# Row statistics in three batches, 16-bit table angles and a filter transform by column halves, in a fused long-convolution and token-mixing kernel

## The chip, the cores and the metric

The kernel runs on one core of one Trainium2 chip. The metric is the device time of one execution in microseconds (us); for the kernel before the change it is the median of six runs.

## What is computed

The reference, cut to what matters (S = 2048 tokens, D = 640 channels, F = 1536 hidden units, inputs in bf16):

```python
x = A_q
g = sigmoid((x * gate_w).sum(-1, keepdims=True))
# branch a: short filter, product, long causal convolution along S by FFT
k_shift = sum_t  k_pad[:, t:t+S, :] * shift_k[:, 3-t]          # 4 taps
kv = k_shift * v
y  = irfft(rfft(kv padded to 2S) * rfft(ssm_k padded to 2S))[:S]
a  = q * (y + kv * ssm_D)
# branch b: a token-mixing MLP on the normalized rows
h = (x - mean(x)) / sqrt(var(x) + 1e-5)                        # over D
u = gelu(einsum("bsd,sf->bdf", h, w1) + b1)
b = (einsum("bdf,fs->bds", u, w2) + b2) transposed to (S, D)
out = g * a + (1 - g) * b
```

## The kernel before, in words

**The convolution.** The Fourier transform along S is done as matrix products with a table `FTB` of cosines and sines, which is made on the chip, and with additions between four residue classes p = 0..3 of the token index ("mixing"). The filter `ssm_k` comes in as channels x tokens. For each half h of the tokens TensorE transposes it in five blocks of 128 channels (`transp`, L841; 8 transposes of 128x128 for each block); ScalarE copies each block from PSUM into `wT` (L853). The forward transform of the filter, `fwd` (L857), then makes for each p and each of two frequency blocks k2 and each component c (cosine or sine) four products of 320 columns: two token blocks kt times two column halves ci. The two column halves lie in the two PSUM banks of a slot `pp`, and ScalarE evacuates both with one instruction of 128x640 into `C[h]` (L871). Since one evacuation covers all 640 channels, the first product needs all five blocks of `wT`. `fwd_even` (L873) does p = 0 and 2 of the second half. Later the same is done for kv (`kv`, L1006, from the transposed keys `KT`), then the products and the inverse transform (`inverse`, L1215).

**The table.** L793 to L814: GpSimd makes small index rows (`acol`, `brow`, and `dif` for the identity matrix `ident`); for each p, VectorE multiplies them into 512 32-bit angles (L806), adds 1024 for the cosine (L807), takes all 1024 angles modulo 4096 (L811), and ScalarE's Sin turns them into 1024 table entries (L813). `ident` is made at L798, the zeroing of `rows` at L799 is GpSimd's, and the `taps` copy at L801 and the small `cw`, `cc` (L822 to L839) bring constants into place. `cw` feeds the four GpSimd products `KF` (L974).

**The MLP.** `X` holds the 2048 rows as 16 tiles of 128x640 (four tiles p in each of four groups hk). For each tile VectorE takes statistics with two instructions of 320 columns and one that joins them (`ln_tile`, L916, rows named `stats` and `mv`); GpSimd turns variances into `rstd` with a power of -0.5 (`ln_scale`, L929); VectorE applies mean and rstd in place (`ln_apply`, L935). This goes in two batches: tiles 0 to 7 are scaled after the statistics of tiles 0 to 11, and tiles 8 to 15 after those of the last four (L959 to L972). The first MLP product (`m1`, L1077) has 12 output tiles ft; each accumulates over hk = 0..3, 8 products of 320 columns for each hk, and reads `X` and a third of w1 in `ring[0]` or `ring[1]`. The second (`m2`, L1115) follows. The memory of `ring[1]` first serves the angles `pint`, the raw keys `kn` and a rearranged copy `kp0`; the keys are rearranged on VectorE and then transposed by DMA into `KT` (`k_turn`, L747), and only after that does the second third of w1 go into `ring[1]`.

**What sets the order.** Nothing runs in the order of the source. `_Sched` (L326) takes each operation with an estimated duration, a priority (by default its place in the source; smaller goes first) and its dependences, plays the engines through, and emits a fixed order for each engine; on the chip each engine executes that order and waits for semaphores in it. `after` adds an order of starts without a wait. There are four PSUM slots, of which convolution work ("cv") may hold three and the MLP ("mlp") two (L335). `m1` and `m2` have the lowest priorities and so fill what the convolution leaves of TensorE. DMAs from SP are issued in one chain. `spin` (L787) puts products of zeros ahead of a step, to keep TensorE busy while it waits.

## Time and profile before

| | us |
|---|---|
| median of 6 runs | 182.64 (181.78 to 182.9) |
| the profiled execution, own time | 181.8 |
| its span, first to last instruction | 180.0 |
| busy: TensorE / VectorE / ScalarE / GpSimd | 173.3 / 171.4 / 116.9 / 43.6 |
| scaling of a tile of X (16 of them), mean of one | 0.444 |
| statistics of 320 columns (32), mean of one | 0.465 |
| filter evacuation 128x640 from PSUM, mean of one | 0.724 |

How to read it: "busy" of TensorE counts products whose ends are modelled and overlap, so a busy TensorE isn't one at its peak. A mean duration is that of one instruction seen alone; instructions in a row overlap a little, so ten evacuations of 0.724 us take 6.07 us. The span leaves out 1.8 us around the program. A row of the timeline has the start, the length, engine, line, output and inputs, the number of instructions merged into it, and in brackets the idle time before it and what ended it.

### The profile page before, as it was taken

The page shows a single profiled execution, that of the slowest core. Times are in us where ns is not written, and L with a number is a line of the kernel's source. Part 1 is how long each engine was busy: PE and PEld are TensorE (multiplying, and loading weights), DVE is VectorE, ACT ScalarE, POOL GpSimd, SP SyncE. Part 2 cuts the span into 40 slices and gives each one's busy share as a digit, 9 for nine tenths or more (in the row PEclk, how much of TensorE's full clock was granted, in tenths as well). Part 3 has the DMA queues.
Part 4 walks back from the last instruction along what each step waited for, and adds up shares of the span by engine and source line. Part 5 has one row for each costly group of instructions (what it writes and reads, how often), then busy time and mean ns, then how long its engine had stood idle before and what let it go on. Part 6 is the DMA issues. An engine that isn't in the chain of part 4 may idle for free.

```text
span 180.0 us, 3335 instructions
## 1 busy us (share of the span) xinstructions
PE 173.3 (96%) x1381; PEld 129.4 (72%) x1381; DVE 171.4 (95%) x203; ACT 116.9 (65%) x176; POOL 43.6 (24%) x42
## 2 busy tenths in 40 slices
PE   7969998999999999999999999999999999999994
PEld 2636786687778677777677778888888887777772
DVE  7999895999999999999999899999999999999984
ACT  5798998899898999616999933132131223753760
POOL 4089404190000054000240110402625000252000
PEclk9999999999999999999999999999999999999999
DMA  6999999999999999998299969798899999599464
GB/s 154 362 410 374 389 302 192 257 410 323 211 260 287 190 270 250 237 221 199 57 240 305 198 85 364 179 209 277 155 197 216 209 201 383 222 152 241 117 225 143
DMA packets 38542, 43.51 MB, mean 242 GB/s; under 512 B 15867, under 2 KB 31360, under 8 KB 38528
## 3 DMA queue, kind: packets, MB, share of 16 engines
q1 hardware_dynamic: 33296, 32.16, 58.4%
q0 software_dynamic: 5200, 11.14, 35.5%
q8 instruction: 11, 0.18, 0.4%
q10 hardware_dynamic: 32, 0.01, 0.0%
q14 instruction: 3, 0.02, 0.0%
HBM read 25.87 MB, written 2.62 MB: 158 GB/s over the span
## 4 chain that ended last, share of the span: by engine, by line
PE 88%; ACT 10%; DVE 0%; issue 0%
PE pp L295 88%; ACT wT L670 3%; ACT C L670 2%; ACT ksh L670 2%; ACT FTB L670 2%; ACT L670 1%; ACT GT L670 0%; DVE O L682 0%; DVE zz L686 0%; ACT cw L670 0%; DVE cst L686 0%
## 5 line engine op out<-in xcount | busy, mean ns | idle before, releaser
L295 PE MATMUL pp<-X,ring 128*128 128x320 bf16 x384 | 55.4, 299 | 0.0
L626 DVE TENSOR_TENSOR C<-C 128x2560 bf16<-128x2560 bf16 (+2 forms) x37 | 54.5, 1524 | 0.0
L295 PE MATMUL pp<-GT,W 128*128 128x320 bf16 x384 | 52.6, 299 | 0.0
L295 PEld LDWEIGHTS pp<-GT,W 128*128 128x128 bf16 x384 | 43.6, 114 | 8.6
L295 PEld LDWEIGHTS pp<-X,ring 128*128 128x128 bf16 x384 | 37.4, 98 | 14.4
L670 ACT ACTIVATE C<-pp 128x640 bf16<-128x640 f32 x64 | 40.4, 724 | 4.7 <-PE pp L295 4.7
L670 ACT ACTIVATE O<-pp,c,omg 128x640 bf16<-128x640 f32 x15 | 13.3, 883 | 34.7 <-PE pp L295 34.7
L264 POOL DMA_DIRECT2D C<-C x8 | 10.9, 1610 | 41.9 <-DVE C L626 38.4
L295 PE MATMUL pp<-wT,FTB 128*128 128x320 bf16 x112 | 17.2, 300 | 2.6 <-ACT wT L670 1.5
L670 ACT ACTIVATE cgb<-pp,gg 128x640 bf16<-128x640 f32 x16 | 12.7, 793 | 5.7 <-PE pp L295 5.3
L295 PEld LDWEIGHTS pp<-wT,FTB 128*128 128x128 bf16 x112 | 10.5, 98 | 7.8 <-ACT wT L670 1.9
L670 ACT ACTIVATE GT<-pp,cc 128x640 bf16<-128x640 f32 x12 | 9.5, 795 | 9.0 <-PE pp L295 9.0
L626 DVE TENSOR_TENSOR tm<-C,C 128x2560 bf16<-128x2560 bf16 (+1 forms) x7 | 14.3, 2059 | 0.0
L922 DVE BATCH_NORM_STATS2 stats<-X 128x6 f32<-128x320 bf16 x32 | 13.6, 465 | 0.0
L295 PE MATMUL pp<-C,FTB 128*128 128x320 bf16 x96 | 13.4, 299 | 0.0
L264 POOL DMA_DIRECT2D C<-q_hi x6 | 5.9, 977 | 27.7 <-DVE C L626 13.2
L295 PEld LDWEIGHTS pp<-C,FTB 128*128 128x128 bf16 x96 | 9.3, 98 | 3.8 <-issue 0.2
L670 ACT ACTIVATE gq<-gq 128x640 bf16<-128x640 bf16 x16 | 11.8, 739 | 0.0
L626 DVE TENSOR_TENSOR SS<-C 128x2560 bf16<-128x2560 bf16 x8 | 11.7, 1488 | 0.1
L626 DVE TENSOR_TENSOR C<-tm 128x2560 bf16<-128x2560 bf16 (+1 forms) x9 | 10.7, 1193 | 0.1
L670 ACT ACTIVATE wT<-pp 128x1024 bf16<-128x1024 f32 x10 | 9.7, 1045 | 1.0 <-PE pp L295 1.0
L670 ACT ACTIVATE ksh<-pp 128x1024 bf16<-128x1024 f32 (+1 forms) x12 | 9.8, 896 | 0.6 <-PE pp L295 0.6
(73 smaller groups left out, 194.2 us busy)
## 6 DMA issues: line engine op xcount, KB each, us to landing
ring<-in_B_w_dram SPq DMA_DIRECT2D x12, 512.0 KB, 7.9
W<-in_B_w_dram SPq DMA_DIRECT2D x12, 512.0 KB, 6.3
C<-C POOLq DMA_DIRECT2D x8, 640.0 KB, 10.5
X<-in_A_q_dram SPq DMA_DIRECT2D x4, 640.0 KB, 8.6
kn<-in_A_k_dram SPq DMA_DIRECT2D x4, 640.0 KB, 9.6
out_dram<-O SPq DMA_DIRECT2D x7, 320.0 KB, 3.4
C<-SS POOLq DMA_DIRECT2D x3, 640.0 KB, 11.6
ssm<-in_A_ssm_k_dram SPq DMA_DIRECT2D x3, 512.0 KB, 7.0
```

The source lines that it names most:

```text
L264: ins = engobj.dma_start(out_ap, in_ap, accum_op=ALU.add, max_dma_last_dim=2560)
L295: ins = self.nc.tensor.matmul(ps_ap, lhsT=lhsT, rhs=rhs, start=start, stop=stop, skip_group_check=True)
L626: o_ = SC.add(eng, d, lambda s: T.op(eng, lambda e: e.tensor_tensor(o, a, b, op), rd, [o]), rd, [o], prio=prio, name="tt")
L670: return T.op("ACT", lambda e: e.activation(o, src, func, **kw), rr + [src], ww)
L922: ops.append(SC.add("DVE", 0.38, (lambda o, i: lambda s: T.op("DVE", lambda e: e.bn_stats(o, i), [i], [o]))(o, i), [i], [o]))
```

## The change

- The angles are made from two 16-bit parts: `tb`, (acol x brow) modulo 4096 and the same plus 1024, made once for all p with 32-bit products of 128 elements, and `jrow`, the rest of the angle for each p and kt, written by eight GpSimd index instructions of 256 elements. For each p there is one 16-bit addition of 1024 elements and one 16-bit modulo of 1024 elements. `pint` becomes 16-bit.
- `ident` is made after the first p's angles; the zeroing of `rows` moves from GpSimd to VectorE; the priorities that held back the Sin of p = 1 and 3 are gone.
- The first half's filter transform (`fwd_c`) runs the column halves outermost: for ci = 0 all p, then ci = 1. The two components c take the two banks of a slot, and one evacuation of 128x640 covers both components of one column half. The counts of products (64) and evacuations (16) stay.
- Row statistics and scaling in three batches, tiles 0 to 7, 8 to 12 and 13 to 15, in one written order on VectorE: statistics of the next batch come before a batch is scaled, and the joining instruction of a tile stands between the two statistics instructions of the next.
- The scheduler's estimates: start times of the engines, DMA rates of the first loads, GpSimd's power (1.75 for 1.05) and index instructions, the transposes; index instructions, memsets and the power no longer take part in its model of the port that VectorE and GpSimd share. The product `sd` x `rstd` loses its priority, and `KF` no longer waits for the last angles.

```diff
--- before.py
+++ after.py
...
@@ -397,9 +400,9 @@
         engs = list(ENGS) + ["SP", "QA"]
         ready = {e: [] for e in engs}
         pend = {e: [] for e in engs}
-        free = {e: 2.4 if e == "ACT" else 0.0 for e in engs}
+        free = {"ACT": 2.93, "DVE": 0.85, "POOL": 0.83, "PE": 1.18, "SP": 0.0, "QA": 0.0}
         port = {"DVE": 0.0, "POOL": 0.0}
-        dma_free = 0.0
+        dma_free = 0.3
         avail = {}
         for op in ops:
             avail[op] = 0.0
@@ -582,8 +585,10 @@
         C = [alloc(f"C{i}", [128, 4, 4, D], BF16) for i in range(4)]
         SS = alloc("SS", [128, 2, 4, D], BF16)
         E_base = cur[0]
-        acol = alloc("acol", [128, 2, 4], I32, at=base_of(SS))
-        brow = alloc("brow", [128, 2, 128], I32, at=base_of(SS) + 64)
+        acol = alloc("acol", [128, 1], I32, at=base_of(SS))
+        brow = alloc("brow", [128, 128], I32, at=base_of(SS) + 64)
+        prod = alloc("prod", [128, 128], I32, at=base_of(SS) + 64 + 2048)
+        tb = alloc("tb", [128, 2, 2, 128], I16, at=base_of(SS) + 64 + 2560)
         dif = alloc("dif", [128, 128], I32, at=base_of(SS) + 64 + 1024)
         dif2 = alloc("dif2", [128, 32], I32, at=base_of(SS) + 64 + 1536)
         KT = [alloc(f"KT{i}", [128, NG, KTW], BF16) for i in range(2)]
@@ -597,7 +602,8 @@
         rows = alloc("rows", [20, 5, 512], BF16, at=base_of(GT))
         kn = [alloc(f"kn{i}", [128, 4, D], BF16, at=base_of(ring[1]) + 5120 * i) for i in range(2)]
         kp = [alloc("kp0", [128, NG, 128], BF16, at=base_of(ring[1]) + 10240), alloc("kp1", [128, NG, 128], BF16, at=base_of(GTB))]
-        pint = alloc("pint", [128, 4, 2, 2, 256], I32, at=base_of(ring[1]))
+        pint = alloc("pint", [128, 4, 2, 2, 256], I16, at=base_of(ring[1]))
+        jrow = alloc("jrow", [128, 8, 256], I16, at=base_of(ring[1]) + 8192)
         W2 = alloc("W2", [128, 32, 512], BF16, at=base_of(ring[0]))
         assert base_of(ring[1]) == base_of(ring[0]) + 16384
         O1 = alloc("O1", [128, 4, 4, D], BF16, at=base_of(X))
@@ -682,8 +688,13 @@
                 return T.op("DVE", lambda e: e.scalar_tensor_tensor(out=o, in0=src, scalar=sc, in1=b, op0=ALU.mult, op1=ALU.add), [src, sc, b], [o])
             return SC.add("DVE", dve_dur(n_of(o), 1), emit, [sc, b], [o], vt=vt, name="fin")
 
+        def nolock(*a, **k):
+            o_ = SC.add(*a, **k)
+            o_.lock = False
+            return o_
+
         def memset(eng, ap, val, prio=None):
-            return SC.add(eng, 0.2, lambda s: T.op(eng, lambda e: e.memset(ap, val), [], [ap]), [], [ap], prio=prio)
+            return nolock(eng, 0.2, lambda s: T.op(eng, lambda e: e.memset(ap, val), [], [ap]), [], [ap], prio=prio)
@@ -727,7 +738,9 @@
             return lambda s: s[:, ci * 512:ci * 512 + 320]
 
         def ssm_load(h, a, b):
-            dma(ssm[:, a:b, 1024 * h:1024 * h + 1024], dr(A_ssm_k, 128 * S * a + 1024 * h, [[S, 128], [128 * S, b - a], [1, 1024]]), 128 * (b - a) * 2048, chain=True, rate=(262.0 if a == 0 else 195.0) if h == 0 else 385.0)
+            dma(ssm[:, a:b, 1024 * h:1024 * h + 1024], dr(A_ssm_k, 128 * S * a + 1024 * h, [[S, 128], [128 * S, b - a], [1, 1024]]), 128 * (b - a) * 2048, chain=True, rate=({0: 262.0, 1: 223.0}.get(a, RL3)) if h == 0 else 385.0)
+
+        RL3 = 394.0
 
         def row8(t, hk):
             return dr(t, (1024 * (hk // 2) + 4 * (hk % 2)) * D, [[8 * D, 128], [1, 4 * D]])
@@ -736,7 +749,7 @@
             return 16 + 128 * (1 - hk % 2)
 
         def x_load(hk):
-            dma(X[:, hk, :, :], dr(A_q, 512 * hk * D, [[4 * D, 128], [1, 4 * D]]), 128 * 5120, chain=True, rate=410.0)
+            dma(X[:, hk, :, :], dr(A_q, 512 * hk * D, [[4 * D, 128], [1, 4 * D]]), 128 * 5120, chain=True, rate=(352.0 if hk == 0 else 415.0))
 
         def w1_load(c, hk):
             dma(ring[c % 2][:, 4 * hk:4 * hk + 4, :], dr(B_w1, 512 * hk * F + 512 * c, [[4 * F, 128], [F, 4], [1, 512]]), 128 * 4096, chain=True)
@@ -790,28 +803,36 @@
         T_PI = float(np.float32(math.pi * (1.0 - 1e-6)))
         memset("DVE", cst[:, 0:1], T_PI)
         memset("DVE", cst[:, 1:2], -0.5)
-        iota = lambda ap, pat, b, cm: SC.add("POOL", 0.2, lambda s: T.op("POOL", lambda e: e.iota(ap, pat, base=b, channel_multiplier=cm), [], [ap]), [], [ap])
-        iota(dif[:, :], [[1, 128]], 0, -1)
-        iota(acol[:, :, :], [[4, 2], [1, 4]], 0, 8)
-        iota(brow[:, :, :], [[-512, 2], [4, 128]], 1, 0)
+        iota = lambda ap, pat, b, cm: nolock("POOL", 0.1 + n_of(ap) / 1100.0, lambda s: T.op("POOL", lambda e: e.iota(ap, pat, base=b, channel_multiplier=cm), [], [ap]), [], [ap])
+        PORD = (0, 2, 1, 3)
+        iota(brow[:, :], [[4, 128]], 1, 0)
+        iota(acol[:, :], [[0, 1]], 0, 8)
+        jr = lambda p, kt: iota(jrow[:, 2 * p + kt, :], [[-512 * (4 * kt + p), 2], [4 * (4 * kt + p), 128]], 4096 + 4 * kt + p, 0)
+        for p in PORD:
+            for kt in range(2):
+                jr(p, kt).dur = 0.34
+            if p == PORD[0]:
+                iota(dif[:, :], [[1, 128]], 0, -1)
         iota(dif2[:, :], [[1, 32]], 128, -1)
-        ts("DVE", ident[:, :], dif[:, :], 0.0, None, ALU.is_equal)
-        memset("POOL", rows[0:20, 3:5, :].rearrange("g a b -> g (a b)")[:, 0:896], 0.0)
+        tt("DVE", prod[:, :], V(acol, 0, [[0, 128]]), brow[:, :], ALU.mult, mode=1)
+        tbv, pr16 = tb[:, 1, :, :], prod[:, :].bitcast(I16).rearrange("q (m t) -> q t m", t=2)[:, 0:1, :].broadcast_to([128, 2, 128])
+        SC.add("DVE", 0.25, lambda s: T.op("DVE", lambda e: e.tensor_scalar(tbv, pr16, 4095, None, op0=ALU.bitwise_and), [prod[:, :]], [tbv]), [prod[:, :]], [tbv])
+        ts("DVE", tb[:, 0, :, :], tb[:, 1, :, :], 1024.0, None, ALU.add, mode=2)
+        memset("DVE", rows[0:20, 3:5, :].rearrange("g a b -> g (a b)")[:, 0:896], 0.0)
         ro, ri = V(rows, 1536, [[128, 4], [160, 4], [1, 32]], pn=20), V(rows, 0, [[1, 4], [0, 4], [4, 32]], pn=20)
-        SC.add("DVE", 0.6, lambda s: T.op("DVE", lambda e: e.tensor_copy(ro, ri), [ri], [ro]), [ri], [ro], prio=0, name="taps")
-        PORD = (0, 2, 1, 3)
         sins = {}
         for p in PORD:
-            pv = pint[:, p, :, 1, :]
-            t_ = tt("DVE", pv, V(acol, p, [[4, 2], [0, 256]]), V(brow, 0, [[0, 2], [1, 256]]), ALU.mult, mode=1)
-            ts("DVE", pint[:, p, :, 0, :], pv, 1024.0, None, ALU.add, mode=2)
-            pa = pint[:, p, :, :, :].rearrange("q a b c -> q (a b c)")
+            pv = V(pint, 1024 * p, [[512, 2], [256, 2], [1, 256]])
+            t_ = tt("DVE", pv, V(tb, 0, [[0, 2], [256, 2], [1, 256]]), V(jrow, 512 * p, [[256, 2], [0, 2], [1, 256]]), ALU.add)
             if p != 0:
                 t_.after.add(pprev)
-            pprev = ts("DVE", pa, pa, 4095, None, ALU.bitwise_and, mode=2)
-            pv3 = pa
+            pa = pint[:, p, :, :, :].rearrange("q a b c -> q (a b c)")
+            pprev = ts("DVE", pa, pa, 4095, None, ALU.bitwise_and, mode=4)
+            if p == 0:
+                ts("DVE", ident[:, :], dif[:, :], 0.0, None, ALU.is_equal)
             sins[p] = act(FTB[:, p, :, :, :, :].rearrange("q a b c d -> q (a b c d)"), pa, ACT.Sin, bias=cst[:, 0:1],
                 scale=-(2.0 * math.pi / 4096.0) * (1.0 - 1e-6), name="sin")
+        SC.add("DVE", 0.6, lambda s: T.op("DVE", lambda e: e.tensor_copy(ro, ri), [ri], [ro]), [ri], [ro], prio=0, name="taps")
 
         for hk in range(2):
             k_load(hk)
@@ -849,10 +870,21 @@
                         items.append((o, ident[0:1, :], Drow[0:1, 128 * db:128 * db + 128], True, False))
                     items.append((o, V(ssm, db * S + 1024 * h + 4 * kt + p, [[8, 128]]), ident[:, :], not dfold, True))
             m_ = mms(vt, (spin(SPIN[db]) if h == 0 else []) + items, name="wtr")
-            m_.dur = 0.5
+            m_.dur = (0.65 + 0.31 * SPIN[db] if h == 0 else 0.55)
             o_ = act(V(wT, 2 * h * SL + 128 * db, [[SL, 2], [D, 4], [1, 128]]), (lambda s: s[:, :].rearrange("q (a b c) -> q a b c", a=2, b=4)), ACT.Copy, vt=vt, name="wT")
             if h == 0:
                 o_.after.add(sins[0 if db == 0 else 2])
+
+        def fwd_c(p, ci, dst, scale):
+            for k2 in range(2):
+                vt = _VT("cv")
+                items = []
+                for kt in range(2):
+                    for c in range(2):
+                        items.append((chk(c), FTB[:, p, kt, c, k2, :], srcW(0)(kt, p, ci), kt == 0, kt == 1))
+                m_ = mms(vt, (spin(WSPIN) if (p, ci, k2) == (PORD[0], 0, 0) else []) + items, name="W")
+                m_.dur = 0.54
+                act(V(dst, p * SL + k2 * D + 320 * ci, [[2 * D, 2], [1, 320]]), two, ACT.Copy, vt=vt, name="We", scale=scale)
 
         def fwd(src, h, p, dst, slot, scale, name, neg=lambda c, k2: False):
             for k2 in range(2):
@@ -929,8 +961,9 @@
         def ln_scale(a, b):
             n = b - a
             ts("POOL", sd[:, a:b], mv[:, a:b, 1], 1e-5, None, ALU.add, prio=0)
-            tt("POOL", rstd[:, a:b], sd[:, a:b], V(cst, 1, [[0, n]]), ALU.pow, prio=0).dur = 1.05
-            return tt("POOL", sd[:, a:b], sd[:, a:b], rstd[:, a:b], ALU.mult, prio=0)
+            o_ = tt("POOL", rstd[:, a:b], sd[:, a:b], V(cst, 1, [[0, n]]), ALU.pow, prio=0)
+            o_.dur, o_.lock = 1.75, False
+            tt("POOL", sd[:, a:b], sd[:, a:b], rstd[:, a:b], ALU.mult, prio=SDP)
 
         def ln_apply(a, b):
             for t in range(a, b):
@@ -940,9 +973,11 @@
 
         MIXP = 330
         LNA = 8
+        SDP = None
         lnlast = []
         kfirst = []
         KFP = (0, 5, 10, 15)
+        WSPIN = 3
         srcW = lambda h: (lambda kt, p, ci: wT[:, 2 * h + kt, p, 320 * ci:320 * ci + 320])
         for h in range(2):
             for db in range(ND):
@@ -951,27 +986,52 @@
                 consts()
             if h in (1,):
                 fwd_even(srcW(h), h, C[h], 1.0 / 1024.0, h == 1, "W")
-            for p in (PORD if h not in (1,) else PORD[2:]):
-                if h == 0 and p in (1, 3):
-                    sins[p].prio = SC.ops[-1].idx - (16.5 if p == 1 else 8.5)
+            if h == 0:
+                for ci in range(2):
+                    for p in PORD:
+                        fwd_c(p, ci, C[0], 1.0 / 1024.0)
+            for p in (() if h == 0 else PORD[2:]):
                 fwd(srcW(h), h, p, C[h], p, 1.0 / 1024.0, "W", (lambda c, k2: False) if h == 0 else (lambda c, k2: c == 1))
             if h == 0:
-                for t in range(8):
-                    ln_tile(t // 4, t % 4)
-                for t in range(8, 12):
-                    ln_tile(t // 4, t % 4)
-                lnlast.append(SC.ops[-1])
-                ln_scale(0, LNA)
-                ln_apply(0, LNA)
-                lnlast.append(SC.ops[-1])
-                for t in range(12, 16):
-                    for o_ in ln_tile(t // 4, t % 4):
-                        o_.after.update(lnlast[-1:])
-                ln_scale(LNA, 16)
-                ln_apply(LNA, 16)
-                lnlast.append(SC.ops[-1])
+                LB = [0, 8, 13, 16]
+                nb = len(LB) - 1
+                seq = []
+
+                def chain(f, *a):
+                    n0 = len(SC.ops)
+                    f(*a)
+                    for o_ in SC.ops[n0:]:
+                        if o_.eng == "DVE":
+                            o_.after.update(seq[-1:])
+                            seq.append(o_)
+
+                pag = []
+
+                def flush():
+                    while pag:
+                        o_ = pag.pop(0)
+                        o_.after.update(seq[-1:])
+                        seq.append(o_)
+
+                def stats_of(k):
+                    for t in range(LB[k], LB[k + 1]):
+                        b0, b1, ag = ln_tile(t // 4, t % 4)
+                        b0.after.update(seq[-1:])
+                        seq.append(b0)
+                        flush()
+                        b1.after.update(seq[-1:])
+                        seq.append(b1)
+                        pag.append(ag)
+                    ln_scale(LB[k], LB[k + 1])
+                stats_of(0)
+                for k in range(1, nb):
+                    stats_of(k)
+                    flush()
+                    chain(ln_apply, LB[k - 1], LB[k])
+                chain(ln_apply, LB[nb - 1], 16)
+                lnlast.append(seq[-1])
                 for g0 in KFP:
-                    tt("POOL", KF[:, g0:g0 + 20 // len(KFP), :, :], V(cw, 7 * g0, [[7, 20 // len(KFP)], [1, 7], [0, 32]]), V(m32, 0, [[0, 20 // len(KFP)], [0, 7], [1, 32]]), ALU.mult, xr=[pv3] if g0 == 0 else []).after.update(kfirst[:1])
+                    tt("POOL", KF[:, g0:g0 + 20 // len(KFP), :, :], V(cw, 7 * g0, [[7, 20 // len(KFP)], [1, 7], [0, 32]]), V(m32, 0, [[0, 20 // len(KFP)], [0, 7], [1, 32]]), ALU.mult).after.update(kfirst[:1])
                     kfirst.append(SC.ops[-1])
                 for hk in range(2):
                     k_turn(hk)
```

More of the change, by code (lines that the diff above doesn't have):

```diff
@@ L12 @@
 I32 = mybir.dt.int32
+I16 = mybir.dt.int16
 ACT = mybir.ActivationFunctionType
@@ L58, in regions @@
         esz_ap = mybir.dt.size(ap.dtype)
+        if space == "PS" and esz_ap != esize:
+            rowsize, esize = rowsize * esize // esz_ap, esz_ap
         assert esz_ap == esize, "bitcast size change unsupported in tracker"
```

## The prediction

> **What bounds the kernel now.** I read the chain of waits in order of time first, since it says where TensorE ever waits:
>
> ```profile
> 1.18 4.39 PE pp L295 x16
> ...
> 5.59 1.02 ACT wT L670
> 6.62 2.08 ACT FTB L670 x2
> 8.69 0.92 ACT wT L670
> 9.61 0.18 ACT cw L670
> 9.79 0.91 ACT wT L670
> 10.70 1.04 ACT FTB L670
> 11.73 1.83 ACT wT L670 x2
> ...
> 13.62 16.40 PE pp L295 x142
> ...
> 41.17 136.12 PE pp L295 x1048
> ```
>
> From 41.17 to 177.31 the chain is TensorE alone, 1048 products without a gap, at their full pace (80 products of `X` in 11.03 us in the timeline: 136 ns each). A change that leaves the products alone, as this one does, can gain only what TensorE loses before 41.17. From 5.59 to 13.57 that chain is ScalarE: five `wT` copies, three Sines and `cw` in a row, while the filter products wait for the fifth `wT`.
>
> The loss, counted: from the end of the first spins (4.35) to 41.17 lie 36.8 us. The timeline has in them 85 transposes and folds (5.8 us), 12 small constants (0.5), 80 filter products (10.9), 56 of `m1` (7.6) and 80 of `kv` (4.3): 29.1 us. So 7.7 us are idle or spins: 5.9 before 13.6, 0.5 from there to 30.95, 1.3 after.
>
> Next, VectorE's timeline, for the row statistics:
>
> ```profile
> 18.77 0.44 DVE L922 BATCH_NORM_STATS2 stats<-X 128x6 f32<-128x320 bf16 x1
> 19.25 0.21 DVE L926 BATCH_NORM_AGGREGATE mv<-stats 128x2 f32<-128x12 f32 x1
> 20.03 2.94 DVE L641 TENSOR_SCALAR X<-X,mv,rstd 128x640 bf16<-128x640 bf16 x8 [0.57 <-POOL rstd L626]
> ...
> 24.07 0.82 DVE L751 COPY kp<-kn 128x2560 bf16<-128x2560 bf16 x1
> ...
> 30.16 2.94 DVE L641 TENSOR_SCALAR X<-X,mv,rstd 128x640 bf16<-128x640 bf16 x8 [2.11 <-POOL rstd L626]
> 33.02 1.49 DVE L626 TENSOR_TENSOR SS<-C 128x2560 bf16<-128x2560 bf16 x1
> ```
>
> VectorE stands 0.57 and 2.11 us in front of the two scalings, waiting for GpSimd's power. Until 30.95, when the third group of `X` is scaled, `m1` has only two output tiles times two groups to give, 32 products. The list of waits of the whole run shows that VectorE waits for nothing else of size; it is 171.4 us busy. It is a second bound just behind TensorE: the last mixing ends at 169.34, behind it 16 inverse products (2.2 us), an evacuation (0.8), and 0.82 + 0.49 + 0.38 + 1.22 on VectorE give 175.2, while the span's last work ends at 177.86. That is 2.6 us of slack, for TensorE ends with 24 products of `m2` (3.42 us at 173.85) that need no more mixing.
>
> **The angles.** Removed on VectorE: 4 x (0.685 + 0.425 + 0.690) = 7.2 us. Added: `prod` of 128 elements, about 0.3 (row of 512 in 32 bits: 0.685, less 384 elements at 1.04 ns, 0.40; a bf16 addition shows 0.52 ns each between 1280 in 0.82 and 2560 in 1.488, at two at a time); the two `tb` operations, 0.45 and 0.3 (rows of 425 ns for 512 and 238 ns for 32); the zeroing of `rows`, 0.5 (`zz`, 256 words, took 0.27; this is 448 words); and for each p an addition and a modulo of 1024 in 16 bits. No row has VectorE adding 16-bit integers. The ends: at the 32-bit product's pace 1024 elements take 1.22 us, at that of the bf16 addition (0.52 ns each and 0.155 fixed) 0.69. The Trainium skill (VectorE: DVE Perf Modes, "What auto-detection actually checks") says that the doubled mode for two inputs asks only for 16-bit elements with a step of one; type bf16 isn't asked for. Both inputs of the new addition run 256 in a row. I take 0.69; by the other end the sum is 2.1 us worse. The modulo: 1024 at the copy's pace (2560 bf16 in 0.82) is 0.42. So 4 x 1.13 + 1.55 = 6.1, a saving of 1.1 us.
>
> GpSimd gets eight index rows. The row `brow` of 256 took 0.34, three in a line start 0.2 to 0.3 apart: first pair done at about 1.8, all at 3.8; VectorE asks for the first at 2.7 and the last at 6.7, so they cost nothing in themselves. Against this speaks a rule of the skill (SBUF — State Buffer, "SBUF: two separate sides"): a VectorE operation in a two-port mode and any GpSimd operation exclude each other for a whole instruction. `ident`, 128 elements beside index rows, took 0.45 where 512 took 0.425: about 0.2 lost. By the rule five such operations before 3.8 could lose 0.3 each, 1.5 us; by the row 0.2 each for two or three. I take 0.5, and the first Sin then starts at 4.0 to 4.4 (before: 3.43), still in ScalarE's idle 1.01 us ahead of 5.59. `ident` is now ready at about 4.4 where the first transpose ran at 4.28: 0 to 0.3 on TensorE, 0.1 taken.
>
> VectorE's preliminaries end at about 8.9 (1.16 + 6.1 + `ident` 0.45 + `taps` 0.4 + the two `dif` 0.5 + 0.3 of overlap lost). `X` cannot be had much sooner: its first statistics ran at 7.89. Two of 32 statistics were done by 9.7 before, 1 to 2 are now: this part is worth 0 to 0.3 us to the statistics.
>
> **The batches.** Sixteen tiles at 0.86 us (starts 11.91, 12.77, 13.63) are 13.7, sixteen scalings at 0.367 are 5.9, two `kp` 1.64. From 8.9: statistics 0 to 7 until 15.8, 8 to 12 until 20.1, scaling 0 to 7 until 23.0, statistics 13 to 15 with one `kp` until 26.4, scaling 8 to 12 until 28.2, `kp` and the rest until 30.1. The power takes about 2.0 us on GpSimd (0.25 + 1.68, and 0.04): the first lies beside five tiles of statistics (4.3), the second beside scaling (2.9), the third beside 1.8 of scaling and `kp`. If that cover were gone, each costs up to 2.0. GpSimd's `KF` (four of 2.06, from about 10) may stand in front of the first; four end by 18.3, so `rstd` by 20.3 at worst, 0.2 late. Mixing thus starts at 30.1 and not 33.02: VectorE gains 2.9 us. The third group is ready at 27.8, not 31.6.
>
> **The column halves.** Counts stay: 64 products, 16 evacuations. What moves is the start. ScalarE from 5.6: three Sines (1.05), three `wT` (0.95), `cw` 0.18: 11.8. The first half's columns lie in three blocks, so the products start at 11.8, not 13.62. In ScalarE's order the two later `wT` (1.9) now fall among 16 evacuations (10 took 6.07, so 9.7) and `cc` 0.2: until 23.6; the second half's five `wT` (4.7) until 28.3, before until 29.16. An evacuation reads two banks in the same shape as before, so its price can go neither way that I see.
>
> **The sum on TensorE.** Until 27.8, 23.45 us after 4.35, it can do 5.8 of transposes, 0.5, 8.7 of filter, 4.35 of `m1` (32): 19.35, and a little of the second half's filter, 0.2. Lost: 3.9. From then on `m1` has three more groups' worth to give (96 products of the first third of w1, 13 us), and the 1.3 us of small losses I leave as they are, for the key transposes, which land near 35.4 with DMA, don't move. Lost in all 5.2 of the former 7.7: 2.5 us gained. VectorE's 2.9 and its 2.6 of slack let it follow. The profiled execution becomes 179.3, its span 177.5; the runs' median stands 0.84 above the profiled one, so 182.64 - 2.5 = **180.1**.
>
> **Rivals.** *All of it (0.15):* ScalarE, now without its idle 1.01, 0.67, 0.45, 0.88 and 0.66, also feeds the second half's filter sooner and the later 1.3 us go as well, with a little of the 3.9: 4 us, 178.6. For: those stalls name ScalarE. Against: KT's DMA.
>
> *Given back at 45 to 65 us (0.22):* the second third of w1 is issued at 49.33, behind key transposes, `kn` loads and `kp`, a chain of DMAs that the change doesn't touch, and lands near 57. Until 58 all work that exists is 53.8 us; a TensorE that lost 5.2 needs it all by 63, and of it half of the first kv transform and the last `m1` tiles come late anyway. If they come as before, 1.5 of the gain turn into waiting: 181.6. For: `m1` is spread thinly there. Against: 24 of its 128 products were left at 58.
>
> *The halves don't do it (0.13):* the fixed order puts Sines or late blocks ahead, or `KF` and the power still stop scaling. Then only one part is left, 1 us or less: 181.9, some of it within what cannot be told from no change.
>
> *Slower (0.10):* the angles. At 1.22 an addition, and each two-port operation held up by index rows, they end at 1.16 + 8.2 + 1.35 + 1.5 = 12.2. The last Sin then stands at 12.2 in ScalarE's fixed order, products of the fourth class and every `wT` behind it come later, and the statistics lose 2.5 us, as much as batching saves. It decides from about 11.5; price 1.5, so 184.1.
>
> *As predicted: 0.40.*
>
> **How the numbers follow.** About 0.3%, 0.55 us, is what a measurement of this kernel can tell from no change. Faster: 0.40 + 0.15 + 0.21 + 0.08 = 0.84; same: 0.01 + 0.04 + 0.02 = 0.07; slower: 0.08 and 0.01 of failing halves, 0.09. The range reaches from 178.4, just under the full gain, to 182.2, past the return of 1.5 and most of the failing halves; the unknown costs (additions 2.1, port 1.0) lie inside.
>
> **What would show it.** Right: 16-bit additions near 0.69 and the last modulo by 8.5; a first filter product of `wT` at 11.5 to 12.2; no wait of VectorE for `rstd` above 0.3; the first mixing at 30; a chain of pure TensorE to the end that has begun with 2.5 us less loss. Wrong: additions at 1.2, `ident` after 4.8 with TensorE waiting, VectorE waiting for `kn` at the first `kp`, TensorE with gaps between 45 and 65, or an end at which inverse products wait for mixing.

## The result and the profile after

The changed kernel takes 179.77 us (median of 8 runs, 179.59 to 180.19), the kernel before 181.88 in the same comparison (17 runs); the ratio is 0.9878 [0.9859, 0.9897], so 2.1 to 2.2 us or 1.2% less. The profiled execution took 180.07, with a span of 178.1 (before 181.8 and 180.0). A second measurement of it, listed below as the control, gave 180.22 and 0.9903 [0.9879, 0.9927].

The chain of waits of the changed kernel, in order of time (start, length, what):

```profile
5.26 9.12 DMA rows<-in_B_b_dram
...
14.43 16.24 PE pp L298 x139
...
30.69 1.30 ACT C L676 x2
...
33.31 0.79 ACT GT L676
34.10 1.20 ACT C L676 x2
...
35.43 139.96 PE pp L298 x1128
```

ScalarE's chain of `wT`, Sines and `cw` has left the front. In its place stands a small DMA, the second of two loads of 3 and 4 KB that bring the biases into `rows`: it was issued at 5.26 and landed at 14.38. From 35.43 to 175.39 the chain is TensorE alone, where before that run began at 41.17 with 1048 products.

TensorE's own timeline shows the first filter products (start, length, engine, line, operation, output and inputs, number merged, idle time before and its releaser). Before the change:

```profile
11.82 0.30 PE L295 MATMUL pp<-wT,FTB 128*128 128x320 bf16 x1
13.62 2.21 PE L295 MATMUL pp<-wT,FTB 128*128 128x320 bf16 x15 [1.50 <-ACT wT L670]
...
30.80 0.45 PE L295 MATMUL pp<-wT,FTB 128*128 128x320 bf16 x2 [0.53 <-ACT C L670]
```

After it:

```profile
5.37 1.33 PE L298 MATMUL pp<-zz 128*128 128x512 bf16 x3
...
11.06 0.72 PE L298 MATMUL pp<-ident,ssm 128*128 128x128 bf16 x8
11.61 0.81 PE L298 MATMUL pp<-zz 128*128 128x512 bf16 x3
12.26 1.79 PE L298 MATMUL pp<-wT,FTB 128*128 128x320 bf16 x12
13.99 0.29 PE L298 MATMUL pp<-ident,rows 4*128 4x4 bf16 x4
14.43 0.18 PE L298 MATMUL pp<-ident,rows 12*128 12x12 bf16 x1 [0.16 <-DMA rows<-in_B_b_dram]
14.54 6.69 PE L298 MATMUL pp<-wT,FTB 128*128 128x320 bf16 x48
```

Before, one product, of the first column half, ran at 11.82 and the next stood 1.50 us for the fifth block of `wT`. So it was not the first product that needed all five blocks, but the first evacuation. In the changed kernel the filter products begin at 12.26 without that wait, and the wait of 0.53 at 30.80, just ahead of the third group of `X`, is gone too. The wait for the biases is short here, 0.16, since 12 filter products and four transposes stand ahead of it. In two more profiles of the same order it is 0.52 (the control) and 0.93 (the kernel with more VectorE work).

ScalarE's timeline:

```profile
3.76 3.36 ACT L676 ACTIVATE FTB<-pint,cst 128x1024 bf16<-128x1024 int16 x3 [0.85 <-DVE pint L646]
7.03 1.00 ACT L676 ACTIVATE wT<-pp 128x1024 bf16<-128x1024 f32 x1
...
9.13 3.76 ACT L676 ACTIVATE wT<-pp 128x1024 bf16<-128x1024 f32 x4
```

Three Sines run back to back, and the first `wT` copy starts at 7.03, where before it started at 5.59. But that does not set the 12.26. The third copy, the last that the first column half needs, ended at 11.07. Behind that moment TensorE's fixed order still has the transposes of the fifth block (11.06) and three spins (11.61). In one of the kernels below (`kp` later) ScalarE made the same copies within 0.01 us of these times, and TensorE has:

```profile
5.14 0.81 PE L298 MATMUL pp<-zz 128*128 128x512 bf16 x3
...
11.75 1.79 PE L298 MATMUL pp<-wT,FTB 128*128 128x320 bf16 x12
```

The same order there began its filter 0.5 us sooner. TensorE's pace in its first microseconds differed: three spins took 0.81 us from 5.14 on, where the changed kernel's profile has 1.33 from 5.37 on.

VectorE's timeline, first the angles, then the scaling:

```profile
2.57 0.69 DVE L632 TENSOR_TENSOR pint<-tb,jrow 128x1024 int16<-128x1024 int16 x1
3.30 0.43 DVE L646 TENSOR_SCALAR pint<-pint 128x1024 int16<-128x1024 int16 x1
...
6.79 0.41 DVE L646 TENSOR_SCALAR pint<-pint 128x1024 int16<-128x1024 int16 x1
8.13 1.28 DVE L954 BATCH_NORM_STATS2 stats<-X 128x6 f32<-128x320 bf16 x3 [0.93 <-DMA X<-in_A_q_dram]
...
19.58 2.23 DVE L647 TENSOR_SCALAR X<-X,mv,rstd 128x640 bf16<-128x640 bf16 x6
23.09 0.83 DVE L764 COPY kp<-kn 128x2560 bf16<-128x2560 bf16 x1 [1.28 <-DMA kn<-in_A_k_dram]
23.83 0.80 DVE L647 TENSOR_SCALAR X<-X,mv,rstd 128x640 bf16<-128x640 bf16 x2
...
28.04 2.89 DVE L647 TENSOR_SCALAR X<-X,mv,rstd 128x640 bf16<-128x640 bf16 x8
30.85 2.88 DVE L632 TENSOR_TENSOR SS<-C 128x2560 bf16<-128x2560 bf16 x2
```

Both waits for `rstd` (0.57 and 2.11 us) are gone. There is a new wait, 1.28 for the raw keys, because the fixed order puts the first `kp` copy ahead of the scaling of tiles 6 and 7. Mixing starts at 30.85 (before 33.02). The angles end at 7.20; VectorE then waits 0.93 for `X`, so what they saved beyond that buys nothing for the statistics.

### The profile page after: what moved, and what is told of

Read it like the earlier page. It is cut to its first block, busy times and chain, and to the rows that moved or that the text cites. A ratio compares the mean times of both kernels' runs of the same rounds, so it can differ in the third digit from the quotient of the medians.

```text
span 178.1 us, 3343 instructions
## 1 busy us (share of the span) xinstructions
PE 173.2 (97%) x1381; PEld 129.7 (73%) x1381; DVE 169.7 (95%) x203; ACT 117.0 (66%) x176; POOL 43.7 (25%) x52
## 4 chain that ended last, share of the span: by engine, by line
PE 88%; DMA 5%; ACT 3%; SPq 2%; issue 0%; DVE 0%
PE pp L298 88%; DMA rows<-in_B_b_dram 5%; SPq L272 2%; ACT C L676 1%; ACT L676 1%; ACT GT L676 0%; DVE O L688 0%
## 5 line engine op out<-in xcount | busy, mean ns | idle before, releaser
L676 ACT ACTIVATE gq<-gq 128x640 bf16<-128x640 bf16 x16 | 11.8, 748 | 0.0
L267 POOL DMA_DIRECT2D O<-q_hi x4 | 4.8, 1200 | 21.3 <-DVE q_hi L632 21.3
```

Source lines behind the costliest of these rows:

```text
L267: ins = engobj.dma_start(out_ap, in_ap, accum_op=ALU.add, max_dma_last_dim=2560)
L676: return T.op("ACT", lambda e: e.activation(o, src, func, **kw), rr + [src], ww)
```

## Experiments

**How they are read.** TensorE's loss at a point is the time since 4.35 less the work done by then (0.1357 us for a product of 320 columns, 0.0675 for a transpose, 0.051 for a key product, 0.04 for a constant, nothing for a spin). Six points are used: the first filter product that reads `wT` (before, and without halves, the second, since one runs ahead and the next waits), the first `m1` product of the third group of `X`, the first key product (kv), the first `m2`, the first inverse product, and TensorE's end.

| kernel | first filter | third group | kv | `m2` | inverse | end | span |
|---|---|---|---|---|---|---|---|
| before | 5.82 | 6.66 | 7.75 | 8.40 | 8.40 | 8.53 | 180.0 |
| changed | 4.59 | 4.99 | 6.39 | 6.61 | 6.63 | 6.63 | 178.1 |
| changed, control | 4.52 | 5.28 | 6.69 | 6.91 | 6.93 | 6.93 | 178.4 |
| without halves | 5.15 | 6.37 | 7.78 | 7.89 | 8.59 | 8.75 | 180.2 |
| two batches | 4.81 | 6.31 | 6.32 | 8.84 | 8.86 | 8.86 | 181.7 |
| 32-bit angles | 5.28 | 6.49 | 7.25 | 8.42 | 8.47 | 8.47 | 181.3 |
| estimates only | 7.95 | 9.28 | 9.29 | 11.17 | 11.18 | 11.18 | 184.0 |
| constants late | 4.66 | 5.57 | 6.97 | 8.00 | 8.01 | 8.01 | 179.5 |
| Sines held | 4.36 | 5.74 | 7.15 | 7.41 | 7.52 | 7.67 | 179.1 |
| all three | 4.77 | 5.49 | 6.25 | 7.56 | 7.69 | 7.70 | 179.1 |
| more VectorE work | 4.42 | 5.57 | 6.98 | 7.20 | 9.44 | 9.59 | 181.0 |
| constants moved | 4.06 | 5.24 | 6.65 | 6.87 | 6.87 | 6.88 | 178.3 |
| `kp` later | 4.06 | 4.69 | 6.10 | 6.32 | 6.33 | 6.33 | 177.8 |
| order mended | 4.76 | 5.63 | 7.04 | 7.26 | 7.28 | 7.28 | 178.7 |

From before to after the loss falls by 1.90 and the span by 1.9. Both kernels make the same products, so that the two agree says only that the 2.7 us behind TensorE's end did not change. Where the loss falls says more: 1.2 at the first filter product, 0.4 more up to the third group; 0.3 is given back by kv, and 0.5 comes behind it.

Three of these profiles have the same order up to 149 us: changed, control and more VectorE work. At the third group they differ by 0.6, so smaller differences between single profiles are not read. They also show what an early wait costs. They waited 0.16, 0.52 and 0.93 for `rows`. The loss at the first filter product and this wait make 4.75, 5.04 and 5.35; the loss at `m2` is 6.61, 6.91 and 7.20, each time 1.85 to 1.87 more. So with nothing else moved the wait is passed on in full.

The first four kernels below, the control and the last three were measured on one chip, the four between on another.

**Theories.** *TensorE theory:* the gain is loss taken from TensorE before about 40 us, and each of the three parts holds a share of it. *Order theory:* the scheduler's new estimates and the order that comes of them do it, and the parts matter little. *VectorE theory:* it is the 2.2 us by which mixing starts earlier. The first four kernels take the changed kernel and put one part, or all three, back to its old form, with a new plan each time.

**The first half's transform without column halves.**

```diff
-            if h == 0:
-                for ci in range(2):
-                    for p in PORD:
-                        fwd_c(p, ci, C[0], 1.0 / 1024.0)
-            for p in (() if h == 0 else PORD[2:]):
+            for p in (PORD if h == 0 else PORD[2:]):
```

> The changed kernel with only the column halves undone: the first filter half goes through fwd again, one evacuation for both halves of a component. TensorE theory (the gain is what TensorE no longer loses before its unbroken run, and the earlier first filter product is most of it): the first product of wT at about 13.8 instead of 12.3, loss up by 1.2 to 1.5, so 181.1 +- 0.3. VectorE theory (the gain is the 2.2 us by which mixing starts earlier): no change, 179.8. Order theory (the corrected estimates give a better fixed order): within 0.3 of 179.8.

Measured: 181.98, ratio to the kernel before 1.0008 [0.9983, 1.0033], so 2.2 above the changed kernel (1.8 above the control). Its TensorE timeline:

```profile
12.00 0.30 PE L298 MATMUL pp<-wT,FTB 128*128 128x320 bf16 x1
12.96 0.58 PE L298 MATMUL pp<-wT,FTB 128*128 128x320 bf16 x3 [0.66 <-ACT wT L676]
```

A product that needs a late block stands and waits for it, as the theory says. It came at 12.96 and not at 13.8, since one product ran ahead. The first four filter products lose 1.0, where the first twelve of the changed kernel lose 0.1. By the third group the loss is 0.8 to 1.4 above the three profiles of the changed order; some of this is a longer wait for `rows`, 0.69. Another 0.7 appears at the first inverse product, where TensorE waits 0.53 for VectorE's `C`; that I had not expected, and with it the time is above the 181.1 expected.

**Two batches of statistics.** The written order is taken out, the loop of before put in:

```diff
-                LB = [0, 8, 13, 16]
...
-                stats_of(0)
-                for k in range(1, nb):
-                    stats_of(k)
-                    flush()
-                    chain(ln_apply, LB[k - 1], LB[k])
...
+                ln_scale(0, LNA)
+                ln_apply(0, LNA)
...
+                ln_scale(LNA, 16)
+                ln_apply(LNA, 16)
```

> The changed kernel with only the row statistics as before: two batches, each scaling behind its own power. TensorE theory: the third group of X is ready about 2 to 3 us later, while until then TensorE has the filter's work; of that 0.4 to 0.8 become loss, 180.4 +- 0.3. VectorE theory: mixing starts 2 us later and so does all else, 181.9. Order theory: within 0.3 of 179.8.

Measured: 183.73, 1.0100 [1.0079, 1.0121], so 3.5 to 4.0 above the changed kernel and 1.8 above the kernel before. VectorE's scalings in its timeline:

```profile
19.37 2.58 DVE L647 TENSOR_SCALAR X<-X,mv,rstd 128x640 bf16<-128x640 bf16 x7 [1.05 <-POOL rstd L632]
...
30.49 2.94 DVE L647 TENSOR_SCALAR X<-X,mv,rstd 128x640 bf16<-128x640 bf16 x8 [2.12 <-POOL rstd L632]
```

Both waits are back. TensorE loses 1.4 from 28.5 to 31.3, just ahead of the third group (waits of 0.53 for `C` and 0.20 for `X`), where the changed kernel loses nothing; by the table the third group stands at 0.7 to 1.3 more. But that is only a part. Between the first key product and `m2` it loses 2.5 where the changed kernel loses 0.2 (waits of 1.07 and 0.40 for ScalarE's `GT`), and then the span has 1.3 more behind TensorE's end. The end of its chain of waits:

```profile
67.93 108.06 PE pp L298 x794
176.02 0.80 ACT cgb L676
176.84 0.84 DVE cgb L632
177.71 0.49 DVE O L632
```

In this plan only 12 `m2` products (1.79 us) were left behind the last inverse product instead of 24 (3.42 us), so the last evacuation and VectorE's last work stand open at the end. The 1.3 goes with the plan: the next two kernels, one of them with three batches, have the same 12 products at the end and the same 1.3.

**Angles in 32 bits.** The table section and the shapes of `acol`, `brow` and `pint` of before are put back (in the diff of the change, the removed lines for the added ones), the estimates stay. The priorities that held two Sines back before the change were not put back, here or in the next kernel.

> The changed kernel with only the 32-bit angles put back, with ident first, the zeroing of rows on GpSimd and the held-back Sines of before. TensorE theory: the Sines come later but wT of the first block earlier; the third wT is about as late or 0.5 later, statistics end 0.5 to 1 later: 180.2 +- 0.4. VectorE theory: VectorE has 1.7 us more work ahead of mixing, 181.3. Order theory: within 0.3 of 179.8.

Measured: 182.72, 1.0032 [1.0013, 1.0051], 2.5 to 3.0 above the changed kernel. The first statistics run at 9.1 (changed: 8.13), mixing starts at 31.8; loss 1.5 to 1.8 more, and the same tail as in the last experiment, 12 `m2` products at the end, 1.3. Of the early loss 0.7 to 0.9 stands already at the first filter product. But in this profile the loads came late: the second load of the filter landed at 7.42 (changed: 6.50, more VectorE work: 6.52) and TensorE waited 0.40 for it, `X` landed at 9.05 (8.10), and `rows` cost a wait of 0.69. The 0.9 at the first filter product is no more than this delay. So what the 32-bit angles themselves cost TensorE is not shown.

**Only the estimates.** All three edits above together; with the estimates stay the Sines' missing priorities and the other small moves of the change.

> All three parts undone; what stays of the change is the scheduler's estimates (start times, DMA rates, lengths of power, transposes and memsets, no lock for the power, no priority for sd x rstd). TensorE and VectorE theories: the time of before, 181.9 +- 0.4. Order theory: most of the gain stays, 180.3 or less.

Measured: 186.09, 1.0211 [1.0182, 1.0240]: 4.2 slower than the kernel before. TensorE's timeline:

```profile
13.75 0.29 PE L298 MATMUL pp<-ident,rows 4*128 4x4 bf16 x4 [1.72 <-DMA rows<-in_B_b_dram]
15.05 0.18 PE L298 MATMUL pp<-ident,rows 12*128 12x12 bf16 x1 [1.02 <-DMA rows<-in_B_b_dram]
...
15.82 8.45 PE L298 MATMUL pp<-wT,FTB 128*128 128x320 bf16 x61
```

With the new estimates and the old parts, the plan puts all five bias transposes ahead of every filter product, TensorE waits 1.72 and 1.02 for their small DMAs, and the filter starts at 15.82. The order theory falls: without the three parts the new estimates, and what stays with them, do harm. The sum of the three single steps back (9.1 against the changed kernel) is more than all three at once (6.3), so they are not separate costs; each has its plan's waits and tail in it, and by the third group each of the three (the last with its late loads) stands at 6.3 to 6.5, near the 6.66 of before.

**Three waits of the changed kernel, taken away in the plan.** The changed kernel shows three early waits: `rows`, the third Sine ahead of the first `wT`, `kp` for `kn`. The question was whether they are paid for at the end, or taken up by a later wait. The first puts the bias transposes (`consts`) behind the transform of the first half:

```diff
-            if h == 0:
-                consts()
...
+                consts()
                 LB = [0, 8, 13, 16]
```

> The changed kernel with the small transposes of b1 and b2 (consts) taken behind the filter products in the source, so that TensorE no longer waits at 13.98 and 14.43 for their load. Theory that this wait is a cost of the changed order: loss down by 0.3 to 0.6, 179.3 +- 0.3, and no wait of TensorE for rows in the list. Rival (the load's wait lies where ScalarE is behind anyway, two evacuations being due): no change, 179.8 +- 0.2.

Measured: 181.32, 0.9971 [0.9960, 0.9982], slower than the changed kernel by 1.1 to 1.6. The wait for `rows` is gone and 64 filter products run in one piece, 12.33 to 21.19. But the first `m1` products went from 21.07 to 23.88, a new wait of 0.23 for `C` came up, and between kv and `m2` the new plan loses 1.0.

The second holds the third Sine back behind the first two `wT`:

```diff
                 o_.after.add(sins[0 if db == 0 else 2])
+                if db < 2:
+                    sins[1 + 2 * db].after.add(o_)
```

> The changed kernel with the Sine of p = 1 put behind the first copy into wT and that of p = 3 behind the second, on ScalarE only (before the change a priority held them back). Theory that three Sines in a row ahead of the first wT (at 7.03, before 5.59) keep TensorE from its transposes: first wT at 5.6, first filter product at 11.8 instead of 12.3, 179.4 +- 0.3. Rival (ScalarE is busy without a gap from 3.76 on, so its order doesn't matter): third wT no earlier, 179.8 +- 0.2.

Measured: 180.81, 0.9944 [0.9929, 0.9959]. The first `wT` copy starts at 5.88, but the third ends at 10.96, hardly sooner than the 11.07 of the changed kernel, as the rival had it. The filter starts at 12.03, within what the same order shows without this edit (11.75 to 12.26), but TensorE then runs into tiles 6 and 7 of `X`, which stand behind the `kp` that waits for the keys. Its timeline:

```profile
25.91 0.45 PE L298 MATMUL pp<-X,ring 128*128 128x320 bf16 x2 [0.82 <-DVE X L647]
```

The third is both together, with `kp` behind the first scaling as well.

> Both of the former, and the first kp kept behind the scaling of tiles 0 to 7, so that VectorE doesn't stand 1.28 us in front of two of them waiting for the keys. TensorE theory: 0.3 to 1.0 less loss, 179.0 +- 0.5. VectorE theory: mixing up to 1.2 us earlier, 178.6. Rival: nothing of this is on the path, 179.8.

Measured: 180.88, 0.9949 [0.9932, 0.9965]. No better. In all three the plan further on also changed, so they say that the edits as a whole don't pay, and not what each wait is worth.

**How far ahead VectorE is.** Two additions of the inverse mixing are executed twice at each of their places (the second repeats the first), 3.0 us more of VectorE; the plan isn't told of it, so the order stays.

```diff
-                tt("DVE", sl(hs, ss + k), sl(hy, sy), sl(hy, sy + 1), ALU.add)
+                o2 = tt("DVE", sl(hs, ss + k), sl(hy, sy), sl(hy, sy + 1), ALU.add)
+                if behind is None:
+                    def twice(s, f=o2.emit):
+                        f(s)
+                        return f(s)
+                    o2.emit = twice
```

> The changed kernel with two of VectorE's additions of 2560 elements ahead of the inverse transform (the first two of invmix for the first half) done twice in place, 3.0 us more work on VectorE at an unchanged order; nothing is left out. TensorE theory: VectorE's slack of 3.3 us at the end takes it, TensorE waits for the first inverse products in the middle but no more work is lost than that wait: 0 to 1 us more, 180.3. VectorE theory: all 3.0 come out at the end, 182.8.

Measured: 182.87, 1.0054 [1.0033, 1.0075], 2.7 to 3.1 above the changed kernel. TensorE's timeline at the first inverse product:

```profile
148.77 1.11 PE L298 MATMUL pp<-GT,W 128*128 128x320 bf16 x7
151.95 8.85 PE L298 MATMUL pp<-C,FTB 128*128 128x320 bf16 x64 [2.06 <-DVE C L632]
160.64 5.60 PE L298 MATMUL pp<-GT,W 128*128 128x320 bf16 x40
```

TensorE waits 2.06 us for `C` while 40 `m2` products that need no mixing lie behind these inverse products in its order. Of 3.0 us, 2.2 come through; VectorE is about 0.8 ahead there. (The other 0.3 to 0.6 is early loss, ahead of the edit, the longer wait for `rows`.)

**The changed kernel's own order, with single instructions moved.** To leave the plan out, the next kernels keep the order that was emitted and move a few entries. First the changed kernel again, as control on the same chip:

> The changed kernel itself once more, beside the next three on the same chip, since the earlier experiments were measured beside the kernel before alone: 179.8 +- 0.3. If it is 180.5 or more here, part of what the experiments lost is the chip's and not theirs.

Measured: 180.22 (179.55 to 181.08, 6 runs), 0.9903 [0.9879, 0.9927].

The bias transposes are moved behind 32 filter products:

```diff
+        od = SC.order
+        cs, ca = [o for o in od if o.name == "cst"][1], next(o for o in od if o.name == "cc")
...
+        od.insert(od.index(ws[8]), cs)
+        od.insert(od.index(we[6]) + 1, ca)
```

> The changed kernel with its fixed order kept, but for the transposes of b1 and b2 and their copy, which are moved behind 32 filter products (before: behind 12). Unlike the run that changed the source, nothing else is planned anew. Theory that the wait at 14 us itself costs: 0.4 to 0.6 less, 179.3. Theory that until the third group of X is scaled TensorE has little left to do anyway, so that an early wait is only passed on to a later one: 179.8 +- 0.2. Theory that the new plan cost the earlier run its 1.5 us: no slower than 179.9.

In this kernel, and in the last one, the copy `cc` came to stand ahead of those transposes on ScalarE, so it copies other data and the two biases aren't the reference's; the amount of work is the same. Measured: 180.22, 0.9909 [0.9890, 0.9929], the control's time. Its TensorE timeline:

```profile
11.74 4.75 PE L298 MATMUL pp<-wT,FTB 128*128 128x320 bf16 x32
17.29 0.29 PE L298 MATMUL pp<-ident,rows 4*128 4x4 bf16 x5 [0.80 <-ACT cc L676]
```

The early products run unbroken, but the displaced `cc` made a wait of 0.80 of its own. So the loss, 0.46 below the control's at the first filter product (not by the move, which lies behind it), is the control's again at the third group. It doesn't show what the biases' wait alone costs.

`kp` behind the scaling of tiles 0 to 7, the order of TensorE and ScalarE as it was:

```diff
                     chain(ln_apply, LB[k - 1], LB[k])
+                    if k == 1:
+                        ap0 = seq[-1]
...
                     k_turn(hk)
+                    SC.ops[n0].after.add(ap0)
```

> The changed kernel with the first kp behind the scaling of tiles 0 to 7 on VectorE; the orders of TensorE and ScalarE stay as they are. Scaling of tiles 6 and 7 comes 1.7 us earlier, the third group of X no earlier than by what of the 1.28 us wait is filled. Theory that VectorE's wait for the keys is on the path: up to 0.8 less, 179.0. Theory that the keys bound it anyway (kp only waits later, behind the scaling): 179.8 +- 0.2.

Measured: 180.02 (179.4 to 181.1), 0.9897 [0.9869, 0.9925]: not to be told from the control. VectorE waits 0.46 and 0.36 for `kn` instead of 1.28, and mixing starts at 30.30. Its profile has 0.6 less loss at the third group than the control's, but 0.46 of that is there at the first filter product already, which this edit can't touch. What is left for it is about 0.1, and a wait for `rows` that is 0.14 shorter accounts for that.

All three moves in the kept order:

> The fixed order of the changed kernel with both of these moves, and the Sine of p = 1 behind the first copy into wT on ScalarE. If early waits of TensorE are on the path: 179.0 or less. If they are passed on until the third group of X: 179.6 +- 0.3. It would be the fastest version if any of the three is worth something.

Measured: 180.56 (180.02 to 182.67, 12 runs), 0.9922 [0.9898, 0.9946]. VectorE now waits 2.1 for `C`, and TensorE 0.75 for `cc`. No version was measurably faster than the changed kernel.

## Why the prediction was right, and where its steps were off

**Right: what bounds it.** TensorE's loss before about 40 us was named as the one thing to gain. Up to 41 us it fell from 8.05 to 6.57, 1.5 of the 1.9. The waits that were named are the ones that went: the 1.50 for the fifth block of `wT`, and VectorE's two for `rstd`.

**Luck: the number.** 179.77 against 180.1 is closer than the working. The profiled execution was put at 179.3, a gain of 2.5, and took 180.07, a gain of 1.7. The median was put 0.84 above the profiled execution, as before the change, and lay 0.30 below it. The two errors largely cancel.

**Right: the angles.** A 16-bit addition of 1024 took 0.69, the value taken, and a modulo 0.43 for 0.42. That agrees with the Trainium skill (VectorE: DVE Perf Modes, "What auto-detection actually checks"), by which 16 bits are asked for and not bf16; by the estimate of 1.22 for the 32-bit pace they would have ended 2.1 later. (0.69 and 0.42 make 1.11, where the sum has 1.13; that is nothing.) The loss of 0.5 to index rows on GpSimd didn't show: `ident` took 0.23 beside them, where a loss was read off its 0.45 of before, and the last modulo ended at 7.20, not 8.5. That the statistics gain little, since `X` isn't there, was right (0.93 of waiting).

**Right: the batches.** No wait for `rstd` is left in this profile. The cover is just enough: where `X` landed sooner, 0.39 (`kp` later) and 0.62 (constants moved) came back. With two batches TensorE loses 1.4 ahead of the third group.

**Off: the first filter product,** 12.26 for 11.8, and for a reason that the sum did not have. It made ScalarE's third `wT` copy the last thing to wait for, at 11.8. That copy ended at 11.07, though the plan put three Sines in front of the first. What came last was TensorE's own order, the fifth block's transposes and the spins, at a pace that differed from one profile to the next.

**Off: the third group,** 29.14 for 27.8. The sum put one `kp` between the scalings and no wait for `kn`; there were two, and the first waited 1.28. Mixing came at 30.85 for 30.1. TensorE paid nothing for it: from 14.54 to 32.4 its loss stays at 5.0.

**Off: the sum.** Loss up to the third group was put at 3.9 and is 4.99: 0.5 more at the first filter product, 0.45 in the next 12 products and the bias transposes, and 0.2 that the sum had lost already (a filter that starts at 11.8 stands for 4.1). The 1.3 behind it is 1.64. Before's full loss is 8.53, not 7.7: the table's prices make it 8.05 at 41.17, where I had stopped counting, and 0.5 lies behind. Of this, 0.8 and not 0.5 lay between 13.6 and the third group. So 7.7 - 5.2 = 2.5 became 8.53 - 6.63 = 1.90; the term that was most wrong is the 3.9.

**Missed: the biases.** The wait for the small DMA of `rows` was not in the prediction. In three profiles of the changed order it is 0.16, 0.52 and 0.93 and is passed on in full; with the old parts (estimates only) it is 2.74. The estimates had no price there at all, and without the parts they cost 4.2.

**Refuted: the slack.** "VectorE's 2.9 and its 2.6 of slack let it follow." The 2.6 were counted at the end, from the 24 `m2` products that need no mixing. The doubled additions show 0.8 at the first inverse product, since a fixed order can't bring those products forward. Before the change there was next to none: the addition that this product reads ended at 150.73 and the product began at 150.91, and where TensorE waited for it (more VectorE work) this step took 0.15. After it they stand at 148.17 and 149.14. So TensorE's gain came through only because VectorE was 2.6 us earlier at that point; VectorE's share is a condition of the gain, not slack.

**Rivals.** Return of the gain between 45 and 65 us did not happen in the changed kernel (0.2 of loss between kv and `m2`, before 0.65); other plans lose more there (two batches 2.5, constants late 1.0), the most of it in two batches at 36.29 already. The full gain of 4 did not come: the loss behind the third group did not shrink, and the filter began no sooner than 12.26. The slower case fell with the additions at 0.69.

**Open.** In the first four kernels the part and its plan can be told apart only by the table, and for the angles not even by that. The spins were left as they are in every kernel: the 13 behind the first block of transposes stand for 3.7 of the 4.59 us that the changed kernel has lost at its first filter product. Whether the filter could begin nearer to the 11.07 of the third copy with fewer of them was not tried.

## What to carry to other kernels

Count the loss of the bound engine up to a few named events, in every kernel of the comparison; where the loss arises tells a part's own effect from that of a new plan, which here was up to 2.5 us in the middle and 1.3 at the end. In a kernel whose order is fixed ahead, slack counted at the end is not slack in the middle. Several profiles of one order are worth having: they show how far a single one can be read (here 0.6 us), and what an early wait costs where nothing else moves (here all of it). Six kernels that took such waits away by another order were still not measurably faster, since each move brought waits of its own.

## What the runs showed of the hardware that was not expected

- A load of 3 or 4 KB, issued at 5.26 behind large ones, landed at 14.38, 9.1 us later.
- TensorE's first seven spins (512 columns) started 0.43 us apart, later ones 0.22, while the granted clock read 1.00 throughout. The quicker pace came after 6.2 in the changed kernel's profile and by 5.1 in that of `kp` later; what sets the moment no run shows.
- GpSimd's power took 1.68 us for 8 elements a partition, 1.35 for 5 and 0.92 for 3: about 0.15 for each and 0.5 fixed.
- Index rows of 256 elements on GpSimd ran beside VectorE's operations without a visible loss on its side: 0.43 for a modulo of 1024 beside them, 0.43 and 0.41 after them.
- The changed kernel's median was 179.77 in one measurement and 180.22 in another, against 181.88 and 181.97 for the kernel before.
